# Split operands of a two-layer expert block: other weight parts, one accumulation bank, and the second token group in parts

## The chip, the cores and the metric

The kernel runs on one core of one Trainium2 chip. The metric is the device time of one execution in microseconds (us), as the median of several runs. Beside it stands one profiled execution with a trace of every engine: PE (matrix products; PEld is its loading of the stationary operand), DVE (vector engine), ACT (scalar engine), POOL, SP (here only a queue that issues transfers), and the DMA engines.

## What is computed

Two blocks in a row, all in float32. The first is a gated linear recurrence over 768 steps for 4 batches and 8 heads of width 48. Its result, as 3072 tokens of width 384, goes through four experts, each a product with w1 (384 x 1024), a relu and a product with w2 (1024 x 384), and the four results are added with weights per token:

```
state = alpha[:, :, t, :, None] * state + einsum('bhd,bhe->bhde', k[:, :, t], v[:, :, t])
y[:, :, t] = einsum('bhd,bhde->bhe', q[:, :, t], state)
...
p = domain_probs / (domain_probs.sum(-1, keepdims=True) + 1e-09)
for e in range(E):
    h = np.maximum(x @ w1[e], 0.0)
    out += p[:, e:e + 1] * (h @ w2[e])
```

## The kernel before

**Work and groups.** The recurrence is done in 24 units of 128 steps of one batch ("attention", L456). A unit leaves 128 tokens. Units are put together in seven groups: group 0 has two units, groups 1 to 5 four, group 6 two. The loop at L987 takes group and expert in turn; the last two groups alternate, expert by expert. For each (group, expert) it calls `up` eight times (L702: one 128-wide slice of the hidden layer, all tokens of the group) and then `down` (L794: the product with w2, per 128 tokens, a "slot").

**Order.** Each engine runs its instructions in the order in which the program writes them. `advance` (L934) puts pieces of the attention of later groups between the products, at times that `deal` (L885) plans from `cost` (L879), a table of what the products should take. `background` (L237) puts in one step of the weight splitting at each call, once per `up` and several times in a `down`.

**Products in parts.** A float32 product on PE is written as two instructions. The kernel avoids this where it can: it writes an operand as two rounded parts, `top` and `low`, and keeps a third, `dif`, from which the mixed terms come in one product. Three products of the rounded kind (fp32r) then stand for one float32 product. `up` works in parts from group 1 on (`split1`, L164). `down` works in parts from group 2 on, and in group 1 for half the hidden slices (tiles) of experts 1 to 3 (`split2`, L165); the rest of group 1, and all of group 0, are float32 products ("whole").

**Banks.** In `up`, six products with parts 1 and 0 go to one PSUM bank (`one`) and three with part 2 to another (`two`, L737). ACT takes `one` out with a factor FINE (L752), DVE adds `two` (L754), ACT makes `top` with the relu (L779), DVE makes `low` (L781), and `dif` is made by DVE during the next `down` (L787). In `down` the terms also have two banks per slot ("sides"), which `add_up` (L851) adds to the result on DVE one after the other, with two tables of weights, `p_fine` and `p_all`. `one`, `two` and the sums of `down` (`ops`) share four banks.

**Splitting weights.** Group 0 uses w1 and w2 unsplit. `split_piece` (L219) makes the three parts of a piece (one fourth of an expert's w1 or w2) with two ACT and two DVE instructions, in three steps, and writes them to DRAM (`kept`) from POOL's queue. Later groups load the parts from there through SP's queue (L196). The 16 pieces of w1 are split while group 0 runs, and the 16 of w2 while group 1 runs: two beside `up` and two in `down` of experts 1 to 3, four in `down` of expert 0. The unsplit w2 pieces lie in a part of the hidden tiles that is not yet in use.

Of the kernel before, what the change touches and what calls it, by code (L numbers as in the profile page):

```python
# [20 lines left out]
def kernel(  # L21
# [57 lines left out]
    FINE = 1 + 1 / 4096  # L79
    TRIM = 1 - 1 / 8192  # L80

# [23 lines left out]
    p_fine = const.tile([P, NBLK, E], F32, name="p_fine")  # L105
# [58 lines left out]
    split1 = lambda gi, e: gi > 0  # L164
    split2 = lambda gi, e, c=0: gi > 1 or gi == 1 and e > 0 and c < NQ // 2  # L165
    makes = [lambda gi, e: gi == 0, lambda gi, e: gi == 1]
# [19 lines left out]
    SPLIT_AT = [(2, 5), (1, 3, 5, 7)]  # L186

    def load_piece(l, i, beside=False):
# [4 lines left out]
        if gi > l:  # L193
            w = wt[l][i] = wts.tile([P, 3, KC * QF], F32R, name=f"w{l + 1}",
                                    bufs=AHEAD if l == 0 else NQ)
            nc.sync.dma_start(out=w.bitcast(F32), in_=kept[l][k])  # L196
            return
        if l == 1 and not beside:
            return
        if l == 0:  # L200

            if gi > 0 or e == 0:
                shared[c] = wts.tile([P, 3, KC * QF], F32R, name="w2", bufs=NQ)
            w = shared[c][:, 2 - e % 2 if gi == 0 else 2].bitcast(F32)
        else:

            place = (hidden[c][:, 0] if not split2(gi, e, c) else hidden[c + NQ // 2][:, 1])
            w = place.rearrange("p f n -> p (f n)")[:, :KC * QF].bitcast(F32)
# [10 lines left out]
    def split_piece(l, i):  # L219
        whole = wt[l][i]  # L220
        w = wts.tile([P, 3, KC * QF], F32R, name=f"w{l + 1}", bufs=AHEAD if l == 0 else NQ)
        top, low, dif = (w[:, part] for part in range(3))

        nc.scalar.activation(out=top, in_=whole, func=ACT.Copy, scale=TRIM)
        yield
        nc.scalar.activation(out=dif, in_=whole, func=ACT.Copy, scale=TRIM * 4096)
        yield
        nc.vector.scalar_tensor_tensor(out=low, in0=whole, scalar=4096.0, in1=dif.bitcast(F32),  # L228
                                       op0=ALU.mult, op1=ALU.subtract)
        nc.vector.tensor_sub(dif, low.bitcast(F32), top.bitcast(F32))  # L230
        nc.gpsimd.dma_start(out=kept[l][i % (E * NQ)], in_=w.bitcast(F32))
        if l == 0:
            del wt[0][i]
        elif split2(1, *divmod(i - E * NQ, NQ)):
            wt[1][i] = w
# [11 lines left out]
    def split_rest(x, out):  # L247
# [3 lines left out]
        nc.vector.scalar_tensor_tensor(out=dif, in0=top.bitcast(F32), scalar=1 / 4096.0,  # L251
                                       in1=low.bitcast(F32), op0=ALU.mult, op1=ALU.subtract)

    def norm_probs():
# [4 lines left out]
        nc.vector.tensor_scalar_mul(out=p_fine, in0=p_all, scalar1=FINE)  # L259
# [442 lines left out]
    def up(gi, e, fc, slots=None):  # L702
# [8 lines left out]
        if fc in ((0, 2) if gi == 1 else (0,)) and begins and gi < 2:  # L711
            half = range(fc, fc + 2) if gi == 1 else range(NQ)
            for k in half:
                load_piece(1, (gi * E + e) * NQ + k, beside=True)
        if gi == 1 and split2(gi, e) and fc in (2, 4):
            making.append(split_piece(1, first_piece(gi, e) + fc // 2 - 1))
        if makes[0](gi, e) and ends and fc in SPLIT_AT[e in (0, E - 1)]:
            k = SPLIT_AT[e in (0, E - 1)].index(fc)
            making.append(split_piece(0, (gi * E + e) * NQ + k))
# [4 lines left out]
        if split1(gi, e):  # L724
# [6 lines left out]
        if not split1(gi, e):  # L731
# [4 lines left out]
        else:  # L736
            two = ps.tile([P, NT], F32, name="two", tag="g", bufs=4)[:, :n]  # L737
            for out, terms in ((one, (1, 0)), (two, (2,))):
                for part in terms:
                    for kc in range(KC):  # L740
                        nc.tensor.matmul(out, lhsT=w[:, part, kc], rhs=x_part(gi, part, kc),  # L741
                                         start=(part == terms[0] and kc == 0),
                                         stop=(part == terms[-1] and kc == KC - 1))

            ends_first = gi < LAST
            for steps in finish:
                for _ in steps if ends_first else [next(steps)]:
                    pass
            ahead = [] if ends_first else list(finish)
            finish.clear()  # L750
            t = work.tile([P, NT], F32, name="t")[:, :n]
            nc.scalar.activation(out=t, in_=one, func=ACT.Copy, scale=FINE)  # L752
            if split2(gi, e, c):
                nc.vector.tensor_add(t, t, two)  # L754
                for steps in ahead:
                    next(steps, None)
                finish.append(hidden_parts(t, parts))
            else:
                nc.vector.tensor_add(whole, t, two)
                finish.append(rectified(whole))  # L760
        while finish and fc == FCH - 1:
            for _ in finish.popleft():
                pass
        background()
        if f == FPQ - 1 and ends:
            if gi == 0:
                for k in range(AHEAD if i == E * NQ - 1 else 0):
                    load_piece(0, i + 1 + k)
# [8 lines left out]
    def hidden_parts(x, parts):  # L777
# [257 lines left out]
```

## Time and profile before

| what | value |
|---|---|
| median of 3 runs | 1047.46 us (1045.82 to 1047.83) |
| the profiled execution, its own time | 1047.06 us |
| its span, first to last instruction | 1045.3 us |
| PE: products in `down`, fp32r / float32 (L834) | 1872 / 288 instructions |
| PE: products in `up` in parts (L741), 512 wide / 256 wide | 1440 / 288 instructions |
| ACT at L752 and L779 | 192 and 172 instructions, 106.9 and 101.8 us |
| DVE at L754, L781, L787 | 172 each, 109.2, 110.4 and 100.6 us |
| DVE, adding up (L863), by p_all and by p_fine into `acc` | 82 and 60 instructions, 49.7 and 35.1 us |

The page gives busy time per engine, the chain of work that ended last, and groups of instructions by line. Other views give the same for a stretch of time (all times count from the first instruction), or list the instructions in order. PE's busy time covers overlaps: products run into each other, so what one costs in a row of equal ones is the distance from start to start, not its listed duration.

### The profile page before, as it was taken

What the parts mean: (1) busy time and instruction counts of PE and PEld (TensorE: products, weight loads), DVE (VectorE), ACT (ScalarE), POOL (GpSimd) and SP (SyncE); (2) the same over time, 40 slices, a digit from 0 to 9 for tenths busy, and PEclk for the clock granted to TensorE, in tenths of its full rate; (3) what the DMA queues carried; (4) which work ended last, traced back from release to release, by engine and by line L of the source; (5) the groups of instructions that cost most, each with busy time, mean ns of one, the idle gap of its engine ahead of it and who ended that gap; (6) DMA issues with size and microseconds to landing.
All of it is one profiled execution on the core that took longest, in us unless ns stands there. A gap on an engine that the chain in (4) does not pass through costs nothing.

```text
span 1045.3 us, 21812 instructions
## 1 busy us (share of the span) xinstructions
PE 1027.5 (98%) x8652; PEld 892.6 (85%) x8652; DVE 774.7 (74%) x1617; ACT 564.9 (54%) x1195; POOL 35.7 (3%) x76
## 2 busy tenths in 40 slices
PE   8889999999999999999999999999999999999998
PEld 7667777687887899898898898898988989898998
DVE  5578787578879868778868777987887875656565
ACT  5687776585666645446456426565465453323232
POOL 2000010000001000000000000000000000000000
PEclk9999999999999999999999999999999999999999
DMA  9497699897868948758768559567595454454531
GB/s 199 142 334 241 190 342 350 315 331 245 273 237 293 372 170 277 309 176 302 280 212 321 200 204 372 196 244 283 167 346 202 161 212 182 181 186 176 212 151 46
DMA packets 145493, 251.67 MB, mean 241 GB/s; under 512 B 107088, under 2 KB 121808, under 8 KB 122864
## 3 DMA queue, kind: packets, MB, share of 16 engines
q1 hardware_dynamic: 138928, 207.88, 58.3%
q0 software_dynamic: 6016, 42.08, 10.1%
q8 instruction: 68, 1.11, 0.4%
q10 hardware_dynamic: 448, 0.33, 0.1%
q14 instruction: 33, 0.27, 0.1%
HBM read 207.80 MB, written 42.47 MB: 239 GB/s over the span
## 4 chain that ended last, share of the span: by engine, by line
PE 88%; ACT 4%; DVE 3%; DMA 3%; issue 1%; SPq 0%; ACTq 0%; DVEq 0%
PE ops L834 37%; PE one L741 23%; PE two L741 11%; PE sc L530 6%; PE yps L625 3%; PE tp L268 3%; PE one L733 2%; ACT qb L504 1%; PE far L586 1%; PE sps L660 1%; DMA w<-kept 1%; DMA rq<-in_q_dram 1%; DMA kept<-w 1%; DVE w L228 1%; DMA rk<-in_k_dram 0%
## 5 line engine op out<-in xcount | busy, mean ns | idle before, releaser
L834 PE MATMUL ops<-w,hT 128*128 128x384 f32 x1872 | 342.8, 340 | 0.2 <-DVE hT L787 0.2
L834 PEld LDWEIGHTS ops<-w,hT 128*128 128x128 f32 x1872 | 322.7, 188 | 3.9 <-ACT t L752 0.7
L741 PE MATMUL one<-xT,w 128*128 128x512 f32 x960 | 251.2, 397 | 1.2 <-DMA w<-kept 0.7
L741 PEld LDWEIGHTS one<-xT,w 128*128 128x128 f32 x960 | 175.9, 188 | 38.8 <-ACT t L752 1.3
L752 ACT ACTIVATE t<-one 128x512 f32<-128x512 f32 (+1 forms) x192 | 106.9, 557 | 174.5 <-PE one L741 169.5
L504 ACT COPY qb<-QT 64x256 f32<-64x256 f32 x322 | 130.9, 407 | 54.5 <-DVE QT L511 30.0
L781 DVE SCALAR_TENSOR_TENSOR hT<-t,hT 128x512 fp32r<-128x512 f32 (+1 forms) x172 | 110.4, 642 | 63.2 <-ACT hT L779 61.7
L754 DVE TENSOR_TENSOR t<-t,two 128x512 f32<-128x512 f32 (+1 forms) x172 | 109.2, 635 | 53.2 <-PE two L741 32.8
L779 ACT ACTIVATE hT<-t 128x512 fp32r<-128x512 f32 (+1 forms) x172 | 101.8, 592 | 86.6 <-DVE t L754 86.1
L741 PE MATMUL two<-xT,w 128*128 128x512 f32 x480 | 135.6, 391 | 0.0
L741 PEld LDWEIGHTS two<-xT,w 128*128 128x128 f32 x480 | 90.0, 188 | 20.2 <-DVE acc L863 0.9
L834 PE MATMUL ops<-hT 128*128 128x384 f32 x288 | 100.6, 491 | 0.1
L787 DVE SCALAR_TENSOR_TENSOR hT<-hT 128x512 fp32r<-128x512 f32 (+1 forms) x172 | 100.6, 634 | 0.0
L540 DVE COPY_PREDICATED near<-masks,sc 128x256 f32<-128x256 uint8 x138 | 73.8, 535 | 24.1 <-PE sc L530 21.4
L511 DVE TENSOR_TENSOR QT<-QT,dec 128x256 f32<-128x256 f32 x135 | 56.8, 421 | 35.6 <-ACT qb L504 35.1
L834 PEld LDWEIGHTS ops<-hT 128*128 128x128 f32 x288 | 52.1, 190 | 29.7 <-DVE acc L863 0.4
L530 PEld LDWEIGHTS sc<-qb,KT 128*64 128x64 f32 x2208 | 69.6, 138 | 8.9 <-issue 4.7
L530 PE MATMUL sc<-qb,KT 128*64 128x64 f32 x2208 | 74.0, 223 | 2.6 <-ACT qb L504 2.6
L863 DVE SCALAR_TENSOR_TENSOR acc<-ops,p_all,acc 128x384 f32<-128x384 f32 x82 | 49.7, 613 | 27.2 <-PE ops L834 26.4
L522 ACT COPY KT<-KT 128x256 f32<-128x256 f32 x138 | 57.5, 416 | 5.1 <-PE sc L530 1.9
L523 DVE TENSOR_TENSOR KT<-KT,dec 128x256 f32<-128x256 f32 x138 | 57.7, 418 | 0.0
L733 PE MATMUL one<-xT,w 128*128 128x256 f32 (+1 forms) x240 | 46.2, 340 | 0.4 <-ACT xT L440 0.4
(125 smaller groups left out, 960.1 us busy)
## 6 DMA issues: line engine op xcount, KB each, us to landing
w<-kept SPq DMA_DIRECT2D x144, 1152.0 KB, 8.0
kept<-w POOLq DMA_DIRECT2D x32, 1152.0 KB, 6.9
hT<-in_moe_w_dram SPq DMA_DIRECT2D x32, 384.0 KB, 6.4
w<-in_moe_w_dram SPq DMA_DIRECT2D x16, 384.0 KB, 6.5
rv<-in_v_dram SPq DMA_DIRECT2D x24, 192.0 KB, 7.6
ra<-in_alpha_dram SPq DMA_DIRECT2D x23, 192.0 KB, 6.3
rq<-in_q_dram SPq DMA_DIRECT2D x23, 192.0 KB, 6.1
rk<-in_k_dram SPq DMA_DIRECT2D x23, 192.0 KB, 6.0
```

The source lines that it names most:

```text
L504: nc.scalar.copy(out=qb[rows, :, i, :].rearrange("p a (b r) -> p a b r", r=m), in_=qv[rows])
L523: nc.vector.tensor_mul(new[:, :, :, 0, :], old[:, :, :, 0, :], spread(halved(decs[li])[:, :, :, 1], m))
L530: nc.tensor.matmul(out[HALF * s:HALF * (s + 1), 2 * p:2 * p + 2, :], lhsT=KTs[li][:, p, HALF * s:HALF * (s + 1)], rhs=qbs[li][:, p, :, QUA ...
L540: nc.vector.copy_predicated(near.rearrange("p a (b two r) -> p a b two r", two=2, r=m)[:, :, :, 1, :], mk.unsqueeze(1).broadcast_to([P, H, ...
L733: nc.tensor.matmul(one, lhsT=w[:, kc], rhs=xraws[gi][:, kc, lo:hi], start=(kc == 0), stop=(kc == KC - 1))
L741: nc.tensor.matmul(out, lhsT=w[:, part, kc], rhs=x_part(gi, part, kc), start=(part == terms[0] and kc == 0), stop=(part == terms[-1] and k ...
L752: nc.scalar.activation(out=t, in_=one, func=ACT.Copy, scale=FINE)
L754: nc.vector.tensor_add(t, t, two)
L779: nc.scalar.activation(out=top, in_=x, func=ACT.Relu, scale=TRIM)
L781: nc.vector.scalar_tensor_tensor(out=low, in0=x, scalar=0.0, in1=top.bitcast(F32), op0=ALU.max, op1=ALU.subtract)
L787: nc.vector.scalar_tensor_tensor(out=dif, in0=top.bitcast(F32), scalar=1 / 4096.0, in1=low.bitcast(F32), op0=ALU.mult, op1=ALU.subtract)
L834: nc.tensor.matmul(sums[at], lhsT=h, rhs=w, start=(n == begins[at]), stop=(n == ends[at]))
```

## The change

The weights are split into other parts: `top` is rounded with LIFT instead of TRIM, and the second part is `both`, which is whole + 4096 * (whole - top); the third is the rest, whole - top. On the other side `dif` becomes top - 4096 * low. The factors FINE fall out, and so the terms of a product add up in one bank:

```diff
-    split1 = lambda gi, e: gi > 0
-    split2 = lambda gi, e, c=0: gi > 1 or gi == 1 and e > 0 and c < NQ // 2
-    makes = [lambda gi, e: gi == 0, lambda gi, e: gi == 1]
+    EARLY = {(1, 2), (1, 3), (2, 2), (2, 3)}
...
+    BESIDE = [{1: 2, 2: 3}, {2: 0, 4: 1}, {2: 0, 4: 1}, {2: 0, 3: 1, 4: 2, 5: 3}]
...
-        if gi > l:
+        if gi > l or gi == 1 and (e, c) in EARLY:
...
-        nc.scalar.activation(out=top, in_=whole, func=ACT.Copy, scale=TRIM)
-        yield
-        nc.scalar.activation(out=dif, in_=whole, func=ACT.Copy, scale=TRIM * 4096)
-        yield
-        nc.vector.scalar_tensor_tensor(out=low, in0=whole, scalar=4096.0, in1=dif.bitcast(F32),
-                                       op0=ALU.mult, op1=ALU.subtract)
-        nc.vector.tensor_sub(dif, low.bitcast(F32), top.bitcast(F32))
+        nc.scalar.activation(out=top, in_=whole, func=ACT.Copy, scale=LIFT)
+        yield
+        nc.vector.tensor_sub(rest, whole, top.bitcast(F32))
+        nc.vector.scalar_tensor_tensor(out=both, in0=rest.bitcast(F32), scalar=4096.0, in1=whole,
+                                       op0=ALU.mult, op1=ALU.add)
...
-            two = ps.tile([P, NT], F32, name="two", tag="g", bufs=4)[:, :n]
-            for out, terms in ((one, (1, 0)), (two, (2,))):
-                for part in terms:
-                    for kc in range(KC):
-                        nc.tensor.matmul(out, lhsT=w[:, part, kc], rhs=x_part(gi, part, kc),
...
-            nc.scalar.activation(out=t, in_=one, func=ACT.Copy, scale=FINE)
-            if split2(gi, e, c):
-                nc.vector.tensor_add(t, t, two)
...
+            for part in (1, 2, 0):
+                for kc in range(KC):
+                    nc.tensor.matmul(one, lhsT=w[:, part, kc], rhs=x_part(gi, part, kc),
+                                     start=(part == 1 and kc == 0), stop=(part == 0 and kc == KC - 1))
+            nc.scalar.activation(out=parts[0], in_=one, func=ACT.Relu, scale=TRIM)
+            while finish:
+                hidden_rest(*finish.popleft())
+            finish.append((one, parts))
...
-        pairs = [slots[k:k + 2] for k in range(0, len(slots), 2)]
-        sides = [[((0, 1), in_parts[:-2]), ((0, 1), in_parts[-2:])], [((3,), whole), ((2,), in_parts)]]
...
+        if gi == 0:
+            steps = [(slot, 3, fc) for slot in slots for fc in tiles]
+        else:
+            pairs = [slots[k:k + 2] for k in range(0, len(slots), 2)]
+            steps = [(slot, part, fc) for parts in ((0, 1), (2,)) for pair in pairs
+                     for part in parts for slot in pair for fc in tiles]
...
-        if slots[0] == 0 and makes[1](gi, e):
-            making.extend(split_piece(1, first + k) for k in range(NQ) if not split2(gi, e, k))
...
+        if gi == 0 and 0 < e < E - 1 and slots[0] == 0:
             making.extend(split_piece(0, first + k) for k in range(2, NQ))
+            making.extend(split_piece(1, first + k) for k in range(NQ) if (e, k) in EARLY)
+        if gi == 0 and e == E - 1 and slots[0] == 1:
+            making.extend(split_piece(1, first + NQ + k) for k in range(NQ // 2))
+        while gi == 1 and (making or splitting):
+            background()
...
-            return 2.1 * n if split1(gi, e) else 2.6 * n
-        return 4.1 if gi > 1 else 4.7 if split2(gi, e) else 5.4
+            return 2.1 * n if gi > 0 else 2.6 * n
+        return 4.1 if gi > 0 else 5.4
```

So ACT takes `top` straight out of the bank, and DVE takes `low` out of the same bank (`hidden_rest`, a scalar_tensor_tensor with max and subtract as at L781); the copy at L752 and the addition at L754 are gone. `down` has one bank per slot, and `add_up` runs once per slot with `p_all`.

Group 1 runs wholly in parts, so it needs all of w2 split in time. Four w2 pieces (the third and fourth of experts 1 and 2: EARLY) are split in the `down` of group 0 and loaded back in group 1. The other twelve are split in group 1, but earlier: pieces 0 and 1 of expert 0 during the last `down` of group 0, the rest beside `up` at the slices that BESIDE names, and whatever is left before `down` begins. A split has two steps instead of three. In group 0, `down` of experts 0 to 2 ends by running all splits that are still open; after group 1 the four w2 loads of the next expert are issued at once, not two of them later. In group 1 the unsplit w2 pieces of experts 1 to 3 lie in a hidden tile of their own turn (`shared["w2"]`), those of expert 0 in part 1 of the tiles of group 0. In SP's queue those of expert 0 stand between the loads of the four w1 pieces for group 1:

```diff
             if gi == 0:
                 for k in range(AHEAD if i == E * NQ - 1 else 0):
+                    load_piece(1, i + 1 + k)
                     load_piece(0, i + 1 + k)
```

## Prediction, made before the changed kernel was run

> **What bounds the kernel now.** I read the page's first part, then the chain, then the groups, then the instructions in order of time in stretches without attention, and last the waits and windows of the early part.
>
> ```profile
> span 1045.3 us, 21812 instructions
> PE 1027.5 (98%) x8652; PEld 892.6 (85%) x8652; DVE 774.7 (74%) x1617; ACT 564.9 (54%) x1195; POOL 35.7 (3%) x76
> ...
> PE 88%; ACT 4%; DVE 3%; DMA 3%; issue 1%; SPq 0%; ACTq 0%; DVEq 0%
> ```
>
> PE sets the end: 88% of the chain. DVE and ACT together hold 7% of it, so work taken from them is worth little unless PE waited for it. What counts is what the products cost from start to start:
>
> ```profile
> 192.55 3.39 PE L834 MATMUL ops<-hT 128*128 128x384 f32 x10
> 195.78 0.60 PE L268 MATMUL tp<-ident,rk 128*128 128x128 f32 x4
> ```
> ```profile
> 905.82 16.81 PE L834 MATMUL ops<-w,hT 128*128 128x384 f32 x96
> 922.46 0.87 PE L741 MATMUL one<-KT,w 128*128 128x256 f32 x6
> ```
>
> The first two lines (PE in order of time, first column the start) give ten float32 instructions in 195.78 - 192.55 = 3.23 us: 0.323 each, and two make a product: 0.646 us. The other two give 96 fp32r products in 922.46 - 905.82 = 16.64 us: 0.1733 each, three of them 0.520. In the same view an `up` of four units takes 889.46 to 905.82 = 16.36 us for 72 products (0.227 each). This `up` and the `down` after it have no attention between them and no wait to speak of: they are PE's floor, and the change keeps their number of products.
>
> **The change, part by part**, against the profiled execution's own 1047.06 us (span 1045.3 and 1.8 around it; the median of the runs shown is 0.4 higher, 1047.46, which I leave aside).
>
> A. *Group 1 in parts.* Of 288 float32 instructions, 2 slots x 8 tiles x 4 experts = 64 products (128 instructions) are group 0's and stay. 80 products go: 4 slots x (8 + 3 x 4) tiles. Each becomes three fp32r products: 80 x (0.646 - 0.520) = 10.1 us less on PE, which is on the path all through group 1 (PE busy 28.3 of 28.3 us in its first `down`). I take -10.1. From below: were the new products held at the weight load's 188 ns, the gain would be 80 x (0.646 - 0.564) = 6.6.
> The row is 0.1733 us for 384 columns. [...]
>
> B. *`up` of the two-unit group.* This one is not at its floor:
>
> ```profile
> 928.47 0.38 ACT L752 ACTIVATE t<-one 128x256 f32<-128x256 f32 x1
> 928.89 0.42 DVE L754 TENSOR_TENSOR t<-t,two 128x256 f32<-128x256 f32 x1 [0.53 <-ACT t L752]
> 928.90 0.97 PE L741 MATMUL one<-KT,w 128*128 128x256 f32 x6
> ...
> 929.34 0.42 ACT L779 ACTIVATE hT<-t 128x256 fp32r<-128x256 f32 x1 [0.49 <-DVE t L754]
> ...
> 929.76 0.38 ACT L752 ACTIVATE t<-one 128x256 f32<-128x256 f32 x1
> ```
>
> Copy, addition and relu follow each other: from one copy to the next 929.76 - 928.47 = 1.29 us, while PE needs 9 x 0.118 = 1.06. With two banks per slice of four, PE soon has to wait: the four such `up`s take 9.03, 9.02, 9.20 and 9.03 us instead of 72 x 0.118 = 8.50. After the change ACT does one instruction (0.38 to 0.42) and DVE one (0.42) per slice, and four slices fit in the banks: -2.1, at most -2.3, at least 0 if another wait takes its place.
>
> C. *Wide `up`s of groups 2 to 5.* The same chain there is 0.60 + 0.69 + 0.63 = 1.9 of 2.04 us, just hidden. It surfaces a few times: gaps of 0.2, 0.1 and 0.1 us around 668, 0.62 and 0.11 at 809, 0.12 and 0.11 at 838; 1.4 us in all. With ACT and DVE relieved (per slice one ACT and one DVE instruction less, 0.6 and 0.69 us) and two slices more of room: -1.2 (0 to -1.4). Everything else that ACT and DVE lose (some 130 us and 150 us) is hidden under PE and counts nothing.
>
> D. *`down` of group 1, other waits.* `w<-kept` 0.9 at 163, 0.3 at 207, and 0.6 and 1.2 more in the second and third mixed `down`s than their products and attention take: 2.9 in all could go. Against it: SP's queue is in order, and each unsplit w2 piece now stands behind a w1 load that waits until a slot of the split buffers has been written out (issues at 148.4, 153.2, 161.4, 165.9). Piece 3 of expert 0 may land at about 170, while its ACT step stands at slice 2 (about 164): ACT would hold for up to 6 us; PE has three slices (6 us) of banks to go on with, and loses 0 to 4. Two more `kept` writes (1.15 MB, 6.9 us landing) fall in a stretch where DMA is at 0.99. In return a split has one ACT step less, so the writes leave some 2 to 10 us sooner. Net -0.5, from -2.9 to +4.
>
> E. *The start of `down`, a new wait.* Before, `down` began with 24 products of tiles 0 to 5, 4.2 us, before it needed tile 7. Now the eighth product needs `top` of tile 7. In the undisturbed stretch the copy starts 0.49 us after the last product of its bank starts (products at 903.78 + 5 x 0.227 = 904.92, copy at 905.40). So `top` starts 0.26 after the `down` and ends at 0.85 or 0.86; tile 7's weight load is due at 7 x 0.173 - 0.19 = 1.02. It fits, by 0.1 to 0.2 us, where ACT is free. Behind that weight load stand all of PE's products. Of the 16 `up`s with attention, the last copy started late in four: 1.74, 1.24, 2.05 and 1.87 us instead of 0.49. In each a relu (0.63, L779 or L791) stood ahead that is gone afterwards; that leaves 0.62, 0.12, 0.93 and 0.75 late, less 0.1 of slack: 2.0 us. Bounds: 0, and 4.5 if nothing is relieved. `low` is due at 23 x 0.173 = 4.0 us and is covered; so are sums of a slot: 24 products (4.2 us) lie between the end of slot 0 and the first `up` product that needs its bank, against 0.61 for `add_up`.
>
> F. *Group 0.* Here PE does wait, and for attention that goes through ACT and DVE:
>
> ```profile
> PE yps L625 <- ACT lat L603: 2.8, 3, 1.4
> PE sc L530 <- ACT qb L504: 2.6, 3, 1.2
> PE far L586 <- ACT qb L504: 1.5, 1, 1.5
> ```
> ```profile
> 59.50:93.90 34.40, 32.01 (x297) 24.83 (x296) 26.70 (x62) 29.04 (x66) 1.60 (x3) 1.00 0.86 268
> 93.90:131.20 37.30, 35.85 (x417) 28.06 (x416) 30.52 (x72) 28.88 (x65) 2.15 (x5) 1.00 0.69 226
> ```
>
> The waits (total, times, longest; 31 to 170 us) make 6.9 us. The windows (length, then busy time of PE, PEld, DVE, ACT, POOL) show ACT at 84% and 77% and DVE at 78% and 82%. The change adds two w2 splits to the `down` of experts 1 and 2: DVE 2 x (0.958 + 0.952) = 3.8 us each time, at its end. It takes one ACT step of 0.84 from every split of w1, 13.4 us over the group, and adds six of 0.84. At worst the whole DVE lag reaches PE twice, +7.6; at best the ACT waits shrink, -4. I take +1.5, nearer to the small end, since both lags have 13 us or more to be worked off.
>
> Unchanged: the last sums and stores, and the start before 20 us. The planner's smaller costs only move attention of group 2 closer together within group 1, as it already stands in group 2.
>
> Sum: -10.1 - 2.1 - 1.2 - 0.5 + 2.0 + 1.5 = -10.4, so 1047.06 - 10.4 = **1036.7 us**.
>
> **Rivals.** *R1, the early splits cost their bounds:* E as taken, F near +6, D near +2, C and B as taken: -10.1 - 2.1 - 1.2 + 2 + 2 + 6 = -3.4, about 1043.5. For it: DVE near 80% and DMA 0.99 just there. Against: writes and splits leave earlier, and twice as many slices of an `up` fit in the banks. *R2, more relief than taken:* A, B, C, D at -2.9, E 0.5, F -4: -19.8, about 1027. For it: PE's waits in group 0 all name ACT, which loses work. Against: those ACT copies mostly wait for DVE in their turn (L504: 30 us behind DVE L511), and DVE gains work there. *R3, slower:* ACT is late with `top` of tile 7 at each `down` with attention. Place: the first products of 16 `down`s. It decides from (10.1 + 2.1 + 1.2 + 0.5 - 1.5) / 16 = 0.78 us each. At the latest copy seen, 2.05 instead of 0.49 less 0.1, it would be 16 x 1.46 = 23.4, and the time 1047.06 - 12.4 + 23.4 = 1058. Against it: only four of 16 were late at all, with more work on ACT than there will be. *R4, the new products don't run at the floor* (188 ns, the weight load): A is 6.6, the time 1040; 96 in a row at 0.1733 speak against it.
>
> **How the numbers follow.** Chances: forecast, 1031 to 1041 with R4 in it, 67%; R1 (1041 to 1047) 15%; R2 (below 1031) 11%; R3 and what acts like it 7%. A measurement of this kernel can tell about 0.2%, 2.1 us, from no change. Faster by more than that: forecast, R2 and most of R1, 90%; within: 4%, the far end of R1 (3%) and a mild R3 (1%); slower: 6%, the rest of R3. Range 1030 to 1044: the forecast and most of R1; it leaves out about 2 in 10: R3, the end of R1, and R2 below 1030. All terms at their upper ends together would give 1047.06 - 6.6 + 4 + 4.5 + 7.6 = 1056.6, all at their lower 1047.06 - 10.1 - 2.3 - 1.4 - 2.9 - 4 = 1026.4; both need every cover to fail or to hold at once.
>
> **What would show it.** A: float32 instructions at the `down` line fall to 128, and group 1 gets about 10 us shorter. B: `up`s of the two-unit group at 8.5 us. C: gaps at 668 and 809 gone. D: no PE wait for `w<-kept`; ACT idle before a split of expert 0's w2. E: idle time of PEld at the line of `down`'s products that names ACT `hT`, in `down`s with attention alone. F: the start of group 1's `up`, now at 158.65. The prediction is wrong if group 1 begins later than 165, or if `down`s of groups 1 to 4 grow by more than 0.8 us each.

## The result, and the profile after

| | before | changed |
|---|---|---|
| median | 1048.07 us (20 runs, 1045.82 to 1049.86) | 1044.99 us (20 runs, 1040.55 to 1048.66) |
| ratio | 1 | 0.9969 (95% interval 0.9959 to 0.998) |
| the profiled execution, its own time | 1047.06 us | 1045.79 us |
| its span | 1045.3 us | 1044.0 us |

The kernel became 3.1 us faster. The forecast was 10.4 us, and the time lies 1 us outside the range. (Of all the runs below, one execution, the profiled one of "the wait filled", had a mean granted clock of 0.848 and took 1130.15 us; it is in that run's median and not in its ratio.) The profile says at once that the engines did what they were meant to do:

```profile
span 1044.0 us, 21240 instructions
PE 1017.8 (97%) x8732; PEld 905.7 (87%) x8732; DVE 639.3 (61%) x1380; ACT 441.5 (42%) x971; POOL 35.6 (3%) x76
...
PE 91%; DMA 2%; SPq 2%; DVE 2%; ACT 1%; issue 1%; ACTq 0%; DVEq 0%
```

PE is busy for 9.7 us less, DVE for 135 and ACT for 123; but the span fell by 1.3. In the last line (the chain by engine) SPq, SP's queue, is new with 2%, some 20 us. The groups by line show PE's new work:

```profile
L809 PE MATMUL ops<-w,hT 128*128 128x384 f32 x2112 | 383.1, 339 | 0.8 <-ACT hT L739 0.8
...
L809 PE MATMUL ops<-hT 128*128 128x384 f32 x128 | 47.5, 505 | 0.0
```

The float32 instructions of `down` (`ops<-hT`, without w) are 128 as said. In order of time (PE alone, first column the start), the two rows that carried the sum before have become these:

```profile
906.55 16.80 PE L809 MATMUL ops<-w,hT 128*128 128x384 f32 x96
923.20 8.64 PE L737 MATMUL one<-KT,w 128*128 128x256 f32 x72
931.68 1.55 PE L809 MATMUL ops<-w,hT 128*128 128x384 f32 x8
```

The 96 products still cost 923.20 - 906.55 = 16.65 us, and the `up` of two units is now one unbroken row of 931.68 - 923.20 = 8.48, its floor. The DVE and ACT side of that `up`, where three operations followed each other, is two steps long:

```profile
928.74 0.38 ACT L739 ACTIVATE hT<-one 128x256 fp32r<-128x256 f32 x1 [0.73 <-PE one L737]
929.16 0.42 DVE L761 SCALAR_TENSOR_TENSOR hT<-one,hT 128x256 fp32r<-128x256 f32 x1 [0.68 <-ACT hT L739]
```

Now both wait for PE, where PE waited for them. So the loss is elsewhere: in the waits of PE between 95 and 200 us (total, times, longest; the three longest of five). `w<-kept` are parts of w1 loaded back from DRAM, `rq` is the q of a unit of attention as it is loaded, and `tp` are its transposes.

```profile
PE one L737 <- DMA w<-kept: 5.0, 2, 3.9
PE tp L267 <- DMA rq<-in_q_dram: 2.2, 1, 2.2
PE tp L267 <- issue: 1.7, 1, 1.7
```

Before, the list for group 0 named ACT three times, and the same stretch, 95 to 200 us, had only 1.4 us for ACT `lat` and 0.7 for `w<-kept`; now DMA stands first. In order of time, these waits stand around the passage from group 0 to group 1:

```profile
161.36 0.78 PE L267 MATMUL tp<-ident,rq 128*128 128x128 f32 x4 [2.20 <-DMA rq<-in_q_dram]
...
165.83 6.37 PE L737 MATMUL one<-xT,w 128*128 128x512 f32 x27 [1.12 <-DMA w<-kept]
...
173.65 6.42 PE L737 MATMUL one<-xT,w 128*128 128x512 f32 x27
183.98 4.18 PE L737 MATMUL one<-xT,w 128*128 128x512 f32 x9 [3.92 <-DMA w<-kept]
```

Group 1 begins at 165.83 instead of 158.65. The last line shows a second loss: nine products of 512 columns take 4.18 us, where 27 of them take 6.42 two lines above (0.227 each). The windows (length, busy time of PE, PEld, DVE, ACT, POOL, then PE's granted clock, the DMA share, GB/s) show why:

```profile
161.60:165.20 3.60, 3.10 (x8) 1.35 (x6) 2.82 (x8) 1.94 (x4) 0.00 (x0) 0.53 1.00 398
165.20:182.10 16.90, 14.24 (x94) 11.43 (x94) 11.01 (x21) 7.36 (x15) 2.68 (x5) 1.00 1.02 409
182.10:189.10 7.00, 5.12 (x14) 4.17 (x15) 6.33 (x13) 5.87 (x14) 0.54 (x1) 0.51 1.09 384
```

Right after the 2.20 us wait, and from within the 3.92 us wait on, the clock granted to PE is half. In the clock's own record the two stretches are 161.70 to 165.11 and 182.18 to 189.01, that is one and two times 3.41 us; before, none lies between 20 and 1043 us. (Each kernel has one more at its start: 16.20 to 19.62 before, ahead of the products of group 0, and 21.75 to 25.17 now, within them.) Behind which waits the clock fell in these traces, and behind which it did not, stands in the last section.

And why is the data late? In all three windows DMA is at 1.00 or more. SP's queue in order of time:

```profile
141.35 16.52 SPq L218 DMA_DIRECT2D hT<-in_moe_w_dram  x1
158.04 1.14 SPq L195 DMA_DIRECT2D w<-kept  x1
...
162.95 0.34 SPq L195 DMA_DIRECT2D w<-kept  x1
```

The issue of one unsplit w2 piece took 16.52 us (second column), and the four w1 loads, issued one by one from 148.4 to 165.9 before, now leave together at 158 to 163. In that time POOL sent writes of split weights. Between 125 and 190 us there are twelve, at 127.43, 131.89, 135.33, 137.19, 139.65, 144.96, 148.93 and 152.22, and again at 168.78, 170.64, 176.53 and 185.53 us, against six before. Twelve times 1152 KB are 14.2 MB, some 35 us of DMA at the 409 GB/s of the second window. From 152 to 156 us the trace has 163 write packets of 9216 bytes (350 ns each) and 492 read packets of 192 bytes (15 ns): 1.50 MB written, 0.09 MB read, while rq, issued at 137.28, waited to come in. Where both queues had packets all the time, from 154 to 156 us, there are 84 write and 86 read packets: one for one in number, and so 0.77 MB were written while 0.02 MB were read.

Late data holds PE in a second way, which the list of waits hides, because it names only the cause that ended last. DVE and ACT in order of time (not all lines):

```profile
179.96 0.84 ACT L231 ACTIVATE w<-hT 128x768 fp32r<-128x768 f32 x1 [6.59 <-DMA hT<-in_moe_w_dram]
...
182.45 0.68 DVE L761 SCALAR_TENSOR_TENSOR hT<-one,hT 128x512 fp32r<-128x512 f32 x1
```

ACT stood 6.59 us in front of the split of the last unsplit w2 piece of expert 0, which landed at 179.94, and the work of `up` behind it in ACT's order stood too. The second line is the instruction that frees the bank for the products at 183.98 (in "the wait filled", below, products at this place wait for just this step); it ended at 183.13. PE had stopped at 180.06, so some 3.1 of its 3.92 us would have been lost even with w in time.

### The profile page after: what moved, and what is told of

Read it like the earlier page. It is cut to its first block, busy times and chain, and to the rows that moved or that the text cites. A ratio compares the mean times of both kernels' runs of the same rounds, so it can differ in the third digit from the quotient of the medians.

```text
span 1044.0 us, 21240 instructions
## 1 busy us (share of the span) xinstructions
PE 1017.8 (97%) x8732; PEld 905.7 (87%) x8732; DVE 639.3 (61%) x1380; ACT 441.5 (42%) x971; POOL 35.6 (3%) x76
## 4 chain that ended last, share of the span: by engine, by line
PE 91%; DMA 2%; SPq 2%; DVE 2%; ACT 1%; issue 1%; ACTq 0%; DVEq 0%
PE ops L809 38%; PE one L737 34%; PE sc L529 6%; PE tp L267 4%; PE yps L624 3%; PE one L731 3%; DMA w<-kept 2%; SPq L218 2%; PE sps L659 1%; PE far L585 1%; ACT qb L503 1%; DMA rk<-in_k_dram 0%; DVE near L539 0%; PE sc L326 0%; SPq L195 0%
## 5 line engine op out<-in xcount | busy, mean ns | idle before, releaser
L809 PE MATMUL ops<-w,hT 128*128 128x384 f32 x2112 | 383.1, 339 | 0.8 <-ACT hT L739 0.8
L809 PEld LDWEIGHTS ops<-w,hT 128*128 128x128 f32 x2112 | 363.8, 188 | 3.0 <-ACT hT L739 1.3
L737 PE MATMUL one<-xT,w 128*128 128x512 f32 x1440 | 348.7, 396 | 5.0 <-DMA w<-kept 5.0
L737 PEld LDWEIGHTS one<-xT,w 128*128 128x128 f32 x1440 | 267.3, 189 | 62.7 <-DVE hT L761 4.5
L739 ACT ACTIVATE hT<-one 128x512 fp32r<-128x512 f32 (+1 forms) x192 | 107.8, 562 | 356.2 <-PE one L737 347.8
L761 DVE SCALAR_TENSOR_TENSOR hT<-one,hT 128x512 fp32r<-128x512 f32 (+1 forms) x192 | 122.6, 645 | 122.9 <-ACT hT L739 122.8
L809 PE MATMUL ops<-hT 128*128 128x384 f32 x128 | 47.5, 505 | 0.0
L731 PEld LDWEIGHTS one<-xT,w 128*128 128x128 f32 x240 | 39.2, 200 | 4.9 <-ACT xT L439 0.6
L737 PE MATMUL one<-KT,w 128*128 128x256 f32 x288 | 34.6, 279 | 0.0
L737 PEld LDWEIGHTS one<-KT,w 128*128 128x128 f32 x288 | 34.4, 188 | 0.0
L624 PE MATMUL yps<-lat,rv 128*32 128x128 f32 x736 | 33.1, 273 | 1.3 <-ACT lat L602 1.3
```

What stands on the lines that cost most here:

```text
L624: nc.tensor.matmul(yps[QUAD * j:QUAD * (j + 1), c, :], lhsT=lhsT, rhs=rhs, start=begins, stop=ends)
L731: nc.tensor.matmul(one, lhsT=w[:, kc], rhs=xraws[gi][:, kc, lo:hi], start=(kc == 0), stop=(kc == KC - 1))
L737: nc.tensor.matmul(one, lhsT=w[:, part, kc], rhs=x_part(gi, part, kc), start=(part == 1 and kc == 0), stop=(part == 0 and kc == KC - 1))
L739: nc.scalar.activation(out=parts[0], in_=one, func=ACT.Relu, scale=TRIM)
L761: nc.vector.scalar_tensor_tensor(out=low, in0=x, scalar=0.0, in1=top.bitcast(F32), op0=ALU.max, op1=ALU.subtract)
L809: nc.tensor.matmul(sums[slot], lhsT=h, rhs=w, start=(n == begins[slot]), stop=(n == ends[slot]))
```

## The experiments

Theory: the early splits' *writes*, and those of expert 0's w2, fill the DMA engines just when group 1's loads are due. Other explanations (rivals): the order of SP's queue; the pace of the splits; their ACT and DVE work (step F of the prediction). Ratios are to the kernel before, timed in the same job.

| run | us (runs) | ratio, 95% interval | start of group 1 | `up` of expert 0, group 1 |
|---|---|---|---|---|
| changed kernel | 1044.99 (20) | 0.9969, 0.9959 to 0.998 | 165.83 | 28.94 |
| w1 loads first | 1049.25 (10) | 1.0014, 1.0005 to 1.0023 | 163.19 | 34.38 |
| no early splits | 1038.18 (4) | 0.9912, 0.9897 to 0.9927 | 157.45 | 31.67 |
| a slower pace | 1051.32 (7) | 1.0039, 1.0027 to 1.0052 | 168.45 | 32.95 |
| no early splits, w1 first | 1044.50 (5) | 0.997, 0.9955 to 0.9985 | 154.70 | 38.56 |
| early writes, no early splits | 1042.63 (6) | 0.995, 0.9935 to 0.9965 | 163.19 | 28.20 |
| early splits, no early writes | 1039.31 (4) | 0.9929, 0.9914 to 0.9944 | 159.26 | 30.78 |
| no early splits, writes moved in the text | 1039.31 (4) | 0.992, 0.9904 to 0.9937 | 155.66 | 32.93 |
| changed, writes moved in the text | 1044.85 (10) | 0.9978, 0.9963 to 0.9992 | 164.25 | 29.57 |
| **no early splits, writes by SP** | **1031.85 (4)** | **0.9841, 0.9828 to 0.9855** | 157.21 | 24.34 |
| changed, writes by SP | 1039.53 (4) | 0.9911, 0.9896 to 0.9926 | 167.19 | 23.98 |
| the wait filled | 1047.19 (11) | 0.9989, 0.9978 to 1.0001 | - | - |
| the wait filled, again | 1047.01 (10) | 0.9997, 0.9986 to 1.0008 | 165.96 | 29.95 |

Each start of group 1 (us from the first instruction of one profile) also holds some luck from the first 27 us, where the half-clock stretch does not lie in the same place (16.20 to 19.62 us before, 21.75 to 25.17 in the changed kernel): the `up` of expert 1 in group 0 begins anywhere from 57.23 to 59.91 us. It begins at nearly the same time in the profiles whose starts are subtracted below: 59.49 before, 59.61 in the changed kernel, 59.70 without early splits.

**w1 loads first.** The queue's order is undone: all w1 loads of group 1 ahead of the unsplit w2 pieces.

```diff
-                for k in range(AHEAD if i == E * NQ - 1 else 0):
-                    load_piece(1, i + 1 + k)
-                    load_piece(0, i + 1 + k)
+                for l in (0, 1):
+                    for k in range(AHEAD if i == E * NQ - 1 else 0):
+                        load_piece(l, i + 1 + k)
```

> The changed kernel with one thing undone: in SP's queue the four w1 loads of group 1 stand ahead of the four unsplit w2 pieces of expert 0, instead of taking turns with them. Theory P (packets): the writes of the splits are bunched, their 9216-byte packets take turns with the read queue's small ones of 192 and 1536 bytes, and so the reads ahead of the w1 loads crawl; the order of the w2 pieces is a small part. Then the waits for rq (2.2 us at 159 to 161) and for the first w1 piece (1.1) stay, the wait of 3.9 us at 180 shrinks by about the 1.2 MB of w2 pieces no longer ahead, 3 us, with the half clock after it: 1039 to 1042. Theory Q (queue order): the w2 pieces in between are the cause; both waits for w1 and both stretches of half clock go: 1033 to 1036. Theory V (vector work): splits in group 0 delay DVE; no change, 1045.

It became slower than the kernel before, outside the ranges of all three theories. The w1 wait did shrink to 1.8 us, but another one grew:

```profile
PE far L585 <- ACT qb L503: 9.9, 1, 9.9
PE tp L267 <- DMA rq<-in_q_dram: 1.9, 1, 1.9
PE one L737 <- DMA w<-kept: 1.8, 1, 1.8
```

PE waits for `qb`, a copy on ACT. ACT in order of time shows that the copy itself was not the problem:

```profile
172.58 0.84 ACT L231 ACTIVATE w<-hT 128x768 fp32r<-128x768 f32 x1 [17.55 <-DMA hT<-in_moe_w_dram]
173.33 0.80 ACT L503 COPY qb<-QT 64x256 f32<-64x256 f32 x2
```

ACT stood 17.55 us in front of the first step of a split whose w2 piece, now last in SP's queue, had not come, and everything behind that step in ACT's order stood with it. So this order moves the wait from w1 to w2, and the wait for rq stays (1.9 us). Of the two orders the changed kernel's is the better; others were not tried.

**No early splits.** The four w2 pieces of experts 1 and 2 that the change splits in group 0 are split in group 1, beside `up`.

```diff
-    EARLY = {(1, 2), (1, 3), (2, 2), (2, 3)}
+    EARLY = set()
-    BESIDE = [{1: 2, 2: 3}, {2: 0, 4: 1}, {2: 0, 4: 1}, {2: 0, 3: 1, 4: 2, 5: 3}]
+    BESIDE = [{1: 2, 2: 3}] + [{2: 0, 3: 1, 4: 2, 5: 3}] * 3
```

> The changed kernel with no w2 piece of experts 1 and 2 split early: all four of each are split in group 1 beside up, at slices 2 to 5, as expert 3's are. Group 0 then writes four pieces (4.7 MB) less. The order in SP's queue stays. Theory P: with two of eight writes gone between 127 and 152 us the read queue gets through; rq and the first w1 piece are in time, the wait at 180 shrinks or goes: 1034 to 1039. Theory Q: nothing changes in the order, so the waits stay: 1043 to 1046. Theory V: two times 3.8 us of DVE work leave group 0, which then ends earlier, by 1 to 3 us, with the waits for DMA still there: 1042 to 1044.

1038.18: some 6 us faster than the changed kernel (0.9912 against 0.9969, intervals apart). Group 1 begins at 157.45. What is left are two waits for w, 6.5 us in all, the longer one of 4.9 for the last w1 piece, with 6.83 us at half clock from 176.1 (mean clock 0.86 from 166 to 180 us and 0.88 from 180 to 192).

**A slower pace.** One empty step more in each split of w1, so that the writes leave later.

```diff
         nc.scalar.activation(out=top, in_=whole, func=ACT.Copy, scale=LIFT)
         yield
+        if l == 0:
+            yield
```

> The changed kernel with one more step in the split of a w1 piece, so that its DVE work and its write come one call later, as in the kernel before; number and size of the writes are the same. Theory P: if bunching by earlier writes is what counts, and not their number, the reads get through between them: 1037 to 1041; if the number counts, 1043 to 1047. Theory Q: no change, 1045. Theory V: the same DVE work somewhat later, 1044 to 1047.

1051.32, slower than before and above every range. The w1 loads of group 1 go out later, the last at 175.22 instead of 162.95, and the waits for w grow from 5.0 to 6.2 us. That group 1 begins 2.6 us later has another place: the `up` of expert 2 in group 0 takes 22.23 us instead of 19.39, with a wait of 2.85 us at its transposes (1.69 in the changed kernel); the mean clock of the execution is 0.991 (0.993 in the changed kernel). So going back to the longer split does not help.

**No early splits, w1 first.** Both edits.

> Both e1 and e2: no early split, and w1 loads ahead of the w2 pieces. Theory P: close to e2, at most 2 us less: 1033 to 1037. Theory Q: as e1, 1033 to 1036; what tells the two apart is e1 and e2 alone. If DMA traffic at the boundary is the whole of the miss, the time comes near 1047.06 less the terms A, B and C that the trace confirms (10.1, 2.1, 1.5), 1033.

1044.50, far above all that was expected (at most 1037); ACT is held as in the first run (PE waits 13.2 us for `qb`) and the gain of taking the early splits out is lost again. The two edits do not add up.

**Early writes without early splits.** Beside "no early splits", four w1 pieces are written twice. The second copies stand where the early w2 writes stood and are overwritten later.

```diff
         nc.gpsimd.dma_start(out=kept[l][k], in_=w.bitcast(F32))
+        if l == 0 and divmod(k, NQ) in {(1, 2), (1, 3), (2, 2), (2, 3)}:
+            nc.gpsimd.dma_start(out=kept[1][k], in_=w.bitcast(F32))
```

> The changed kernel without its four early splits (as in the run that took them all out, 1038.2), but with four writes more: the w1 pieces 2 and 3 of experts 1 and 2 are written twice, the second time into the places of the early w2 pieces, from the same tiles and at the same time. So the early writes are there, without the ScalarE and VectorE work of the early splits. Theory (the writes of the early splits hold up the loads for group 1): about 1044 to 1046, with group 1 beginning near 165 us, the wait for rq and half-clock stretches on TensorE as in the changed kernel. Rival (it is the early splits' ScalarE and VectorE work that costs): 1038, group 1 beginning near 157.5.

1042.63, 1.4 us short of the theory's range and well above the rival's 1038. Stage by stage it is clean: the `down` before group 1 takes 19.91 us (19.88 in the changed kernel, 13.56 without early splits), with a wait again, this time for an unsplit w2 piece of group 0:

```profile
PE one L739 <- DMA w<-kept: 5.3, 2, 3.9
PE ops L811 <- DMA hT<-in_moe_w_dram: 2.5, 1, 2.5
```

The second copies also hold their buffers longer, so this run alone does not tell full DMA engines from late buffers. The load of rq ahead of group 1 does, since once it is issued it needs no more buffer: from its issue to its landing it took 24.0 us in the changed kernel, 22.8 here, 11.5 without early splits, and 6.8 in the next run.

**Early splits without early writes.** The counterpart: the four pieces are split early too, but the result is neither written nor used.

```diff
-            making.extend(split_piece(1, first + k) for k in range(NQ) if (e, k) in EARLY)
+            making.extend(split_piece(1, first + k, keep=False) for k in range(2, NQ))
...
-        nc.gpsimd.dma_start(out=kept[l][k], in_=w.bitcast(F32))
+        if keep:
+            nc.gpsimd.dma_start(out=kept[l][k], in_=w.bitcast(F32))
```

> The counterpart: w1 pieces written once; w2 pieces 2 and 3 of experts 1 and 2 are split in group 0 with the same ScalarE and VectorE operations, but their results are not written and not used (group 1 splits all four pieces beside its own products, as in the run without early splits). So the early vector work is there without the writes. Theory (writes): about 1038 to 1039, group 1 beginning near 157.5 to 158.5. Rival (vector work): 1044 to 1046, group 1 beginning near 165.

1039.31, 0.3 us above the theory's range and far below the rival's. The `down` before group 1 takes 13.56 again. The vector work has a price of its own: the `up` of expert 2 in group 0 takes 19.41 us instead of 17.51, and its one wait is the 1.7 us for `tp` named `issue` that the changed kernel's list shows too.

The two runs split the late start of group 1 almost without a rest: 19.91 - 13.56 = 6.35 us from the writes, 19.41 - 17.51 = 1.90 from ACT's and DVE's work, together 8.25; between the changed kernel and "no early splits" it is 165.83 - 157.45 = 8.38.

**Writes moved in the text.** The four writes of expert 0's w2 are put off until `down` of expert 0, once without and once with the early splits.

```diff
-        nc.gpsimd.dma_start(out=kept[l][k], in_=w.bitcast(F32))
+        keep = lambda: nc.gpsimd.dma_start(out=kept[l][k], in_=w.bitcast(F32))
+        if i in range(E * NQ, E * NQ + NQ) and l == 1:
+            held.append(keep)
+        else:
+            keep()
...
+        while held:
+            held.popleft()()
```

> No early splits, and the four writes of expert 0's split w2 (161.99 to 179.83 us in the run without early splits) are held back until the products of down of expert 0 in group 1 begin, when the w1 loads that group 1 waits for have landed. Nothing else moves. Theory (the writes share the DMA engines with the w1 loads, packet for packet): the wait of 4.9 us for w before the last quarter of up of expert 0, and with it the 6.8 us at half clock (worth 3.4 us), go: 1030 to 1033. Rival (the wait comes from SP's queue alone, in which the w1 loads are issued late behind the unsplit w2 pieces and rk): the wait stays over 3 us and the time stays at 1037 to 1039. A third outcome: the writes, held back, then delay the next loads and the time is given back in expert 1: over 1036 with the wait for w in another place.

> The changed kernel with its early splits and writes, and the four writes of expert 0's split w2 held back until down of expert 0 in group 1 begins. Theory (packets of writes against loads): the wait of 3.9 us for w at 180 us shrinks to under 2, and the 6.8 us at half clock behind it (3.4 us) go; the wait for rq at 159 us and the 3.4 us at half clock after it stay, since the early writes before 158 us cause them: 1038 to 1041. Rival (SP's issue held up alone): no change, 1043 to 1047.

1039.31 and 1044.85: no change, but the edit did not do what it says, and so it judges nothing. POOL issued the writes at 160.21, 162.08, 168.96 and 177.98 us; without the edit it was 161.99, 164.26, 170.34 and 179.83. Counted from the start of group 1 (155.66 and 157.45) that is the same within 0.5 us. Here the later place in the text delayed nothing: POOL had nothing else to wait for.

**Writes by SP.** The same four writes, issued by SP, whose queue stands behind the loads at that place.

```diff
-        keep = lambda: nc.gpsimd.dma_start(out=kept[l][k], in_=w.bitcast(F32))
+        keep = lambda: (nc.sync if i in range(E * NQ, E * NQ + NQ) and l == 1 else nc.gpsimd).dma_start(out=kept[l][k], in_=w.bitcast(F32))
```

> The run with deferred writes and no early splits moved the four writes of expert 0's split w2 only in the order of the text: GpSimd, which issues them, had nothing else to wait for and issued them at 160.2, 162.1, 169.0 and 178.0 us, about where they were. Here SyncE issues them, at the start of down of expert 0, behind the loads that SyncE issues there (178 to 185 us). Theory (the DMA engines are full, and the first two writes, 2.36 MB, take some 5.6 us of them at 420 GB/s ahead of the last w1 load): the wait of 4.9 to 5.6 us for w before the last quarter of up of expert 0 shrinks to under 1, the 6.8 us at half clock behind it (worth 3.4 us) go, and the time is 1030 to 1033. Rival (the loads are late for another reason: issued late, or held by the small packets of rk): wait over 3 us, 1037 to 1040. Third outcome: the writes hold up expert 1's w1 loads instead, with a wait for w near 210 us.

> The changed kernel, early splits and writes included, with the four writes of expert 0's split w2 issued by SyncE at the start of down of expert 0 in group 1. Theory: the wait at 180 us and its half clock go (about 3.9 and 3.4 us), the delay before 166 us stays, because the early writes cause it: 1037 to 1040. Rival: no change, 1043 to 1047.

1031.85 and 1039.53, both where the theory puts them. Without early splits SP's queue reads:

```profile
160.82 6.89 SPq L174 DMA_DIRECT2D rk<-in_k_dram  x1
...
171.48 6.81 SPq L196 DMA_DIRECT2D w<-kept  x4
178.38 1.86 SPq L237 DMA_DIRECT2D kept<-w  x4
```

The writes start at 178.38. The last packet of expert 0's last w1 piece came in at 171.00; with the writes from POOL it was 177.82, in the changed kernel 183.06. ACT's wait for the last unsplit w2 piece fell too, from 7.07 us without early splits to 1.26. The whole list of PE's waits between 95 and 200 us is

```profile
PE one L742 <- DMA w<-kept: 1.4, 1, 1.4
PE sc L534 <- issue: 0.8, 1, 0.8
```

and the clock is at 1.00 in all of four windows that cover 140 to 192 us (0.998 over the whole span). This version is faster than both kernels, by 16.6 us against the one before. With the early splits kept, the wait at 180 us goes, and what is left stands ahead of group 1 (3.1 us for w, 1.7 for rq, 1.7 for `qb`, with a mean clock of 0.995 over the span): the early writes are still there. The edit moves the writes in time and to another queue at once; whether a late write from POOL's queue would do as well was not tried.

**The wait filled.** Eighteen products more in the changed kernel, just ahead of those that wait 3.9 us; their results are overwritten.

```diff
+            for _ in range(18 if gi == 1 and e == 0 and fc == 6 else 0):
+                x = x_part(gi, 1, 0)
+                nc.tensor.matmul(one, lhsT=x[:, :P], rhs=x, start=True, stop=True)
```

> The changed kernel with 18 products more on TensorE (fp32r, 512 columns, about 227 ns each, 4.1 us), into the bank of the seventh up of expert 0 in group 1, just ahead of the products that wait 3.9 us for w at 180 us; their results are overwritten. Theory (the half clock follows from TensorE standing still): the wait is filled, the 6.8 us at half clock from 182.3 us go, and the time falls by about 3 us beside the changed kernel, to 1041 to 1042, though work was added. Rival (the half clock has another cause, or its stretch comes anyhow): the time stays at 1045 or rises.

> The changed kernel with the 18 products more in the wait at 180 us once again, for a profile of it at the full clock; the run before measured 1047.2 beside 1048.4 of the kernel before, so no gain over the changed kernel. Theory (the half clock follows from TensorE standing still, and the time did not fall because something else is late behind the filled wait): no half clock near 182 us, and the wait for w before the last quarter of up of expert 0 is gone or short, but another wait or a later landing of w makes up for it. Rival (the half clock comes anyhow): 3.4 or 6.8 us at half clock between 178 and 190 us in spite of the products. Third outcome: the wait for w is longer than the 4.1 us of the added products, since the landing of w does not depend on them, and TensorE still stands still for over 2 us.

1047.19 and 1047.01: 2 us more than the changed kernel, not 3 less. The profile of the second run shows why:

```profile
183.35 4.38 PE L737 MATMUL one<-xT 128*128 128x512 f32 x18 [1.51 <-DVE hT L764]
187.57 2.21 PE L740 MATMUL one<-xT,w 128*128 128x512 f32 x9
```
```profile
166.60:170.20 3.60, 3.60 (x11) 2.78 (x10) 3.53 (x4) 1.45 (x3) 0.53 (x1) 0.53 1.03 416
170.20:195.90 25.70, 24.19 (x244) 19.69 (x242) 15.96 (x34) 13.23 (x28) 2.69 (x5) 1.00 0.99 374
```

The added products waited 1.51 us for their bank, behind the hold of ACT described above, and then ran until 187.57. The last packet of w had come in at 183.21; in the changed kernel the products start 0.92 us after it, so w could be used from about 184.1 on, and the filler was some 3.4 us too long. Behind it the clock is full (nine products in 2.21 us instead of 4.18), and between 166.60 and 195.90 us the only half-clock stretch is the one behind the earlier waits (0.53, then 1.00). That fits a half clock that follows from PE standing still, but this pair does not show it: in this execution PE came to the place at 181.84 instead of 180.06, and would have stood only some 2.3 us without the added products.

## Why the prediction failed, by its own steps

- **A, right.** The `down`s of experts 1 and 2 in group 1 fell by 1.98 and 2.61 us (16 products each: 2.02 by the rate taken, and in the second the wait of 0.6 named in D). Experts 1 to 3 together fell by 7.95; 2.03 of it are 64 attention products that moved into group 2, which leaves 5.9, against 48 x 0.126 = 6.0. Expert 0's 4.0 are in the product count too, but are covered by the waits: its `up` and `down` went from 48.46 to 49.65. In the version with SP's writes they take 45.04, 3.4 less.
- **B and C, right.** The four `up`s of the two-unit group take 8.48 each, -2.4 in all (-2.1 taken), with 0.4 more from `down`s that were not counted. The three wide `up`s named fell by 0.43, 0.75 and 0.31: -1.5 (-1.2 taken).
- **E, right in kind, too dear.** PE's products waited for `hT` twice, 0.8 us in all, both in one `down` with attention (at 322 us); +2.0 was taken.
- **F, the step that failed.** The start of group 1 was said to move by +1.5 and moved by +7.2. The step priced the early splits as DVE and ACT work, bounded at 7.6, and that part was measured at 1.9, near the value taken. The four writes, which the step did not have, are 6.35 us in the run with them alone. Against both stands that group 1 begins 1.2 us earlier than before where neither is there: 1.9 + 6.35 - 1.2 = 7.05. That 7.2 lies inside the step's bound is luck, since the bound was for DVE's lag. And the 1.2 is a net figure: the first `up` of group 0, into which the half-clock stretch of the start falls in the changed kernel (21.75 to 25.17), takes 11.77 us there and 11.52 without early splits, 10.45 before. In "no early splits, writes moved in the text" it takes 10.44, and group 1 began 3.0 us earlier than before.
- **D, wrong in sign.** It saw "two more `kept` writes" beside DMA at 0.99 (between 125 and 190 us there are six more, twelve against six), and took it as a relief that "the writes leave some 2 to 10 us sooner". They do: the four writes of expert 0's w2 left at 168 to 186 instead of from 195 on. That put them among the w1 and w2 loads for expert 0, whose last packet came in only at 183.06. With 4.0 for A taken off, expert 0 became 5.2 us longer instead of 0.5 shorter; the upper bound was +4. The hold of ACT that the step priced at 0 to 4 us did come, larger than thought: piece 3 of expert 0's w2 landed at 179.94 and not at about 170, ACT stood 6.59 us for it, and some 3.1 us of PE's wait are covered by it. So the step had this path right and the landing wrong: it took the loads' landing as free of the new writes. (A small misreading: its first wait for w, put at 0.9, is 0.7 in the list of waits before.)

Against the profiled span the places add up: +7.2 (start of group 1), +1.2 (its expert 0), -5.9 (its experts 1 to 3), +0.4 (group 2, beside the moved attention), -1.5 (C), -2.8 (B with the `down`s) are -1.4; the span fell by 1.3.

Of the 13.2 us by which the changed kernel is longer than the best version until expert 0 of group 1 is done, 1.9 are the ACT and DVE work, 5.8 more waits for DMA (7.2 against 1.4) and, as an estimate from half of the time that PE worked at half clock, (164.71 - 161.70) / 2 + (189.01 - 183.98) / 2 = 4.0, the clock (the first stretch as far as PE worked in it, to the wait of 1.12 before 165.83). Of the other 1.5, 0.7 is a wait of PE for `qb` on ACT ahead of group 1, and 0.4 stood there already when expert 1 of group 0 began; the rest I cannot place.

Rival R1 had nearly the time (1043.5), by luck and with the wrong mechanism: it put +6 on the same step as DVE lag. R3 and R4 did not occur. The sign that was named, group 1 beginning later than 165 us, did come true.

## What to carry to other kernels

Where DMA is at 0.99 in a stretch, as here, a transfer that leaves sooner may be no relief but go ahead of something: list every read that is due in that stretch, and count the bytes of the new writes against them. Here background writes did best behind the loads of the next stage, on a queue that has to wait for those loads; moving them in the program's text alone did nothing, since their engine had nothing else to wait for. A list of waits names only the cause that ended last: look for a second one just behind it. And a wait of PE may have a half-clock stretch behind it, to be counted too: in the changed kernel the one of 2.20 us had 3.41 us behind it, the one of 3.92 had 6.83.

## What the runs showed of the hardware

- PE's granted clock fell to one half behind some waits and not behind others. In the changed kernel the wait of 2.20 us that ended at 161.36 went with 3.41 us at half clock (161.70 to 165.11), the one of 3.92 that ended at 183.98 with 6.83 (182.18 to 189.01). Without early splits one of 4.9 went with 6.83 from 176.1, and in the second run of "the wait filled" one of 3.67 that ended at 165.96 with a clock of 0.53 from 166.60 to 170.20. In "no early splits, writes by SP" a wait of 1.40 that ended at 163.17 had none behind it (1.00 from 158 to 180 us). In the changed kernel with writes moved in the text one of 1.89 that ended at 159.16 had none (1.00 from 159.64 to 163.05), nor had one of 3.17 that ended at 164.25: the 27 products behind it take 6.49 us, as at full clock (6.42 in the changed kernel). So the length of the wait alone does not decide in these runs.
- In the changed kernel's trace the half-clock stretches begin at 21.75, 161.70 and 182.18 us, which are 41 and 6 times 3.41 us apart. Cut into windows of 3.41 us that begin there (and at 16.20 in the kernel before), the two traces have two windows at full clock between 30 and 1030 us in which PE stood idle for more than 1.48 us: 2.20 from 158.29 and 2.12 from 178.77, both in the changed kernel. Half clock follows these two and no other. In these two lines PE's busy time is the second number; the first window is followed by half clock, the second, with most of the 3.17 us wait, is not:

```profile
158.29:161.70 3.41, 1.21 (x6) 0.56 (x5) 1.18 (x3) 0.00 (x0) 0.00 (x0) 1.00 1.07 355
159.64:163.05 3.41, 1.44 (x6) 0.56 (x4) 2.12 (x4) 1.82 (x4) 0.00 (x0) 1.00 0.93 356
```

  (The first is the changed kernel, with PE idle for 2.20 us; the second the one with writes moved in the text, idle for 1.97, and 1.20 us of that wait fell into the next window.) Of the changed kernel's half-clock windows the one from 182.18, with 1.80 us idle, was followed by a second; those from 161.70 (0.41 idle) and 185.60 (none) were followed by full clock. Idle time is not the whole measure: in the kernel before, half clock followed the window from 12.79 us, with 1.19 idle, and did not follow the one from 33.27, with 1.48.
- The issue of a load on SP takes 0.38 us in the median of the changed kernel's trace. Two took 16.52 and 14.33 us (from 141.35 and 165.76), in stretches in which POOL sent writes of 9216-byte packets (at 144.96, 148.93 and 152.22; at 168.78, 170.64 and 176.53), and the next in SP's queue left only behind them, at 158.04 and 180.19. The second of them, rk, took 13.1 us without early splits, and 6.9 where the writes of expert 0's w2 were moved to SP.
